# Reordering the second group of an attention-plus-MLP kernel: when a pair's mean, the weights' splits and the gates' multiplication are queued

## The chip, the cores and the metric

The kernel runs on one core of one Trainium2 chip. The metric is the device time of one execution in microseconds (us), the median of several runs. The profile is one execution of the program on the chip, taken by the hardware profiler. Its engine names are used here: PE is TensorE, DVE is VectorE, ACT is ScalarE, SP issues nearly all the transfers. Each engine works through its own instructions in the order in which the program lists them.

## The reference

```python
batch, n_heads, seq, head_dim = (8, 8, 576, 64)      # q, k, v
n_tokens, d_model, d_ff = (4608, 512, 2048)

kv  = np.einsum('bhsd,bhse->bhde', k, v)             # no softmax: 64 x 64 per head
out = np.einsum('bhsd,bhde->bhse', q, kv)
rms = np.sqrt(np.mean(out * out, axis=-1, keepdims=True) + 1e-06)
x   = out / rms * g_norm                             # then (B,H,S,D) -> (B*S, H*D)

h  = x @ w_in
sp = np.maximum(h, 0.0) + np.log1p(np.exp(-np.abs(h)))   # softplus
g  = h * erf(sp)                                     # "the gates"
y  = g @ w_out
```

Attention without a softmax gives each head a 64 x 64 matrix, an RMS norm follows, and the result is the input of a two-layer MLP. `w_in` and `w_out` arrive as 64-bit floats and are turned into 32-bit ones on the chip.

## The kernel before, in words

**Tiling.** The tokens are worked in nine groups T = 0 to 8 of 512: the first 512 tokens of each of the eight batch entries, and at last the 8 x 64 tokens left over. The hidden dimension is cut into 16 blocks (`FC`) of 128. The heads are taken as four pairs p = 0 to 3 (`NP`), a pair filling 128 partitions. While the MLP of group T runs, the attention of group T + 1 is worked in pieces between its matmuls.

**Steps.** The first two groups (`FIRST`) go through a loop of steps n = 0 to 32; T, f = divmod(n, 16). A step makes the hidden block f of its group ("the product of the step"), takes it out of PSUM, starts its softplus, and then multiplies an older block, n - 5 (`LAG`), by `w_out` into four PSUM banks ("the projection", `project`, L502). Erf runs once in four steps (f = 3, 7, 11, 15) for four blocks, since softplus and erf need different ACT tables. The later groups go through another loop, which the change does not touch.

In the second group (T = 1, n = 16 to 31) the product changes its kind from f = 2 on (`hidden`): eight matmuls of x's upper and lower parts go into a bank `n_ps`, four of a sum of both into `m_ps`. ACT copies `n_ps` with a scale to `h` (L684, "the gates' copy"), DVE adds `m_ps` to it (L427, "the add"), ACT takes the softplus (L686). `n_ps` and `m_ps` are the same two banks in every step (`turns=False`), so the next step's product can't start before the copy has read `n_ps`, nor reach its last four matmuls before the add has read `m_ps`. "The gates' multiplication" `hs[done] * ss[done]` (L644, done = n - 4) is on DVE; the projection of the next step is the first to need it.

**Weights' splits.** The second group also cuts the weights into three parts each for the later groups: `w_upper` on ACT (L411) in step f for two or three blocks (`to_cut`), `w_lower` on DVE (L414, L417) a step later, then a store to DRAM from the SP queue.

**Pieces of the attention.** For each pair, `attention` gives six pieces:

- products: kv on PE (L281), transposes of q (L303); DVE copies kv to `bd_kv` (L296), ACT copies q (L304)
- apply: q times kv on PE (L309); ACT squares it (L312)
- halve: DVE splits the squares in two (L322, L323), for group 2 and later; sq_hi and sq_lo
- mean: matmuls with a matrix of 1/64 (L330, L331; in group 1 L335); ACT loads the table of Ln and Exp (L105), Ln, Exp, Square (L342 to L344), then loads the softplus table (L108)
- norm: three DVE instructions (L350, L353, L362)
- split: x into three parts, one instruction on ACT (L387), two on DVE (L390, L393), for group 2 and later

**What sets the order.** The order is written out by hand (`manual_schedule`): an engine's queue is the order of the program. `pieces_of(T)` puts each piece in one of three places of a step: 0 is ahead of the step's product, 1 is behind softplus and the weights' cutting but ahead of the projection, 2 is behind the projection. The PSUM pool `ps_at` has two banks, which kv, the transposed q, `se_ps` and the means take in turn: the next pair's products need what the previous pair's norm has read.

In the first group the DVE also turns the 64-bit weights into 32-bit ones (`w_split` L197, L206, `w_join` L216, L220, L230).

Of the kernel before, what the change touches and what calls it, by code (L numbers as in the profile page):

```python
# [44 lines left out]
ALU = mybir.AluOpType  # L45
# [5 lines left out]
BATCH = 4  # L51
# [3 lines left out]
FIRST = 2  # L55
# [5 lines left out]
def kernel(  # L61
# [10 lines left out]
    nc = tc.nc  # L72
# [6 lines left out]
    NP = H // 2  # L79
    KC = DM // P  # L80
    FC = DF // P
# [61 lines left out]
    for i in range(2):  # L143
        nc.gpsimd.dma_start(
            out=g_col[i * D : i * D + D, :], in_=g_norm.rearrange("(d one) -> d one", one=1)
# [94 lines left out]
    def w_next(what):  # L240
        i = w_at[what]
        if i < len(w_order):
            w_at[what] = i + 1
            {"load": load_w, "split": w_split, "join": w_join}[what](*w_order[i][1:])

    def weights():

        w_next("split")
        w_next("join")
        w_next("load")  # L250
# [162 lines left out]
    def lower_w(x, high, low, both):  # L413
        nc.vector.scalar_tensor_tensor(  # L414
            out=low, in0=high.bitcast(FP32), scalar=SHIFT, in1=x, op0=ALU.mult, op1=ALU.subtract
        )
        nc.vector.tensor_tensor(  # L417
            out=both, in0=high.bitcast(FP32), in1=low.bitcast(FP32), op=ALU.subtract
        )
# [33 lines left out]
    w_kept, w_new, w_now = {}, {}, {}  # L453
# [19 lines left out]
    def w_lower(which, f):  # L473

        t, x, parts = w_new.pop((which, f))
        lower_w(x, *(parts[:, i] for i in range(3)))
        kept = w_kept[which, f] = dram.tile([P, 3, G], FP32, name=f"w_{which}{f}")
        for i in range(3):
            if t is None:
                nc.sync.dma_start(  # L480
                    out=kept[:, i].rearrange("p (c f) -> p c f", c=KC), in_=parts[:, i].bitcast(FP32)
                )
        if t is not None:
            nc.sync.dma_start(out=kept, in_=t.bitcast(FP32))
            if which == "in" and f >= WHOLE:
                w_now[which, f] = [t]
# [94 lines left out]
    def pieces_of(T):  # L581

        steps = [([], [], []) for _ in range(FC)]
        for p in range(NP):
            products, apply, halve, mean, norm, split = attention(T, p)
            short = T < FIRST or p == NP - 1
            f = (BATCH - 1) * (p + 1) if T < FIRST else BATCH * p
            steps[f][1].append(products)  # L590
            steps[f + 1][1].append(apply)
            steps[f + 2][0].append(halve)
            with_erf = short and (f + 2) % BATCH == BATCH - 1

            place = 2 if T < FIRST and p == 0 else 1 if short else 0
            steps[f + 3 - short][place].append(partial(mean, table=not with_erf))
            steps[f + 4 - short][0].append(norm)
            steps[f + 5 - 2 * short][0].append(split)
        return steps


# [11 lines left out]
    hs, ss, plain = {}, {}, {}  # L613
    whole = FIRST * FC - BATCH

    def due(k):

        i = w_at["join"] + k
        ahead = 1 if LAG - 2 <= n < LAG + BATCH else 2
        return i < len(w_order) and w_order[i][0] <= n + ahead  # L620

    for n in range(FIRST * FC + 1):
        T, f = divmod(n, FC)
        if n == FC:
            early_room.close()
            late = ctx.enter_context(tc.tile_pool(name="late", bufs=1))
            x_new = ctx.enter_context(tc.tile_pool(name="x_new", bufs=1))
            acc = ctx.enter_context(tc.tile_pool(name="acc", bufs=1))
            w_in_p = ctx.enter_context(tc.tile_pool(name="w_in_p", bufs=BATCH))
            low = low_room.enter_context(tc.tile_pool(name="low", bufs=1))  # L630
            forms = late.tile([P, 3, KC, G], FP32R, name="x_forms0")
            x_forms[FIRST] = [forms[:, i] for i in range(3)]
        if T < FIRST:
            if f == 0:
                steps = pieces_of(T + 1)
            if due(1):
                weights()
            for piece in steps[f][0]:
                piece()
        while due(0):  # L640
            weights()
        done = n - LAG + 1
        if 0 <= done < whole:
            nc.vector.tensor_tensor(out=hs[done], in0=hs[done], in1=ss[done], op=ALU.mult)  # L644
        if T == FIRST - 1:
            if f == 0:
                x_high = wide.tile([P, KC, G], FP32R, name="x_high", tag="h")
                x_low = low.tile([P, KC, G], FP32R, name="x_low")
                for i in range(0, KC, 2):
                    upper(xT[T][:, i : i + 2], x_high[:, i : i + 2])  # L650
                for i in range(0, KC, 2):
                    lower_only(xT[T][:, i : i + 2], x_high[:, i : i + 2], x_low[:, i : i + 2])
            for key in list(w_new)[:2]:
                w_lower(*key)
        if T == FIRST - 1 and f >= WHOLE:
            n_ps, m_ps = hidden(T, f, turns=False)
        elif T < FIRST:

            if n > 1:
                plain[n] = ps_h.tile([P, G], FP32, name="h_ps", tag="h")  # L660
                blocks = [(n, c) for c in range(KC)]
            elif n == 0:
                for i, (pool, tag) in enumerate(((ps_at, "at"), (ps_o, "o0"))):
                    plain[i] = pool.tile([P, G], FP32, name="h_ps", tag=tag)
                blocks = [(i, c) for c in range(KC - 1) for i in range(2)] + [(0, KC - 1)]
            else:
                blocks = [(1, KC - 1)]
            for i, c in blocks:
                nc.tensor.matmul(  # L669
                    plain[i],  # L670
                    lhsT=w_in_sb[:, c, i % FC * P : i % FC * P + P],
                    rhs=xT[T][:, c, :],
                    start=(c == 0),
                    stop=(c == KC - 1),
                )
        if T < FIRST:
            if n == whole:
                old_h = acc.tile([P, BATCH, G], FP32, name="h", tag="e")
            h = hs[n] = old_h[:, n - whole] if n >= whole else unit("h_sb")
            s = ss[n] = unit("s_sb")  # L680
            if n in plain:
                nc.scalar.copy(h, plain.pop(n))
            else:
                nc.scalar.activation(h, n_ps, AF.Copy, scale=SHIFT - 1.0)  # L684
                add(h, m_ps)
            nc.scalar.activation(s, h, AF.Softplus)  # L686
            if T == FIRST - 1:
                if f == 1:
                    x_both = wide.tile([P, KC, G], FP32R, name="x_both", tag="h")
                    for i in range(0, KC, 2):  # L690
                        both_only(x_high[:, i : i + 2], x_low[:, i : i + 2], x_both[:, i : i + 2])
                    x_forms[T] = x_high, x_low, x_both
                for key in list(w_new):
                    w_lower(*key)
                for key in to_cut[f]:
                    w_upper(*key)
            if n == 0:
                w_next("split")
            for piece in steps[f][1]:
                piece()  # L700
            if f % BATCH == BATCH - 1:
                for i in range(n - BATCH + 1, n + 1):
                    nc.scalar.activation(ss[i], ss[i], AF.Erf)
                softplus_table()
            if T == FIRST - 1:
                load_parts("in", {FC - 3: 2, FC - 2: 1, FC - 1: 1}.get(f, 0))
        if n >= LAG:
            T2, f2 = divmod(n - LAG, FC)
            last = n - LAG in (FC - 1, whole - 1)
            project(f2, hs[n - LAG], last)  # L710
            if last:
                sums(*((acc, "e") if T2 < FIRST - 1 else (wide, "h")))
                if T2 == 0:
                    for j in range(J):
                        store(T2, j, es.pop(j))
        if T < FIRST:
            for piece in steps[f][2]:
                piece()
    for n in range(whole, FIRST * FC):
        nc.vector.tensor_tensor(out=hs[n], in0=hs[n], in1=ss[n], op=ALU.mult)  # L720


    low_room.close()
# [41 lines left out]
    for m in range(first_batch, batches + 1):  # L765
        T, b = divmod(m, NB)
# [8 lines left out]
        def piece():  # L775
            if todo:
                todo.pop(0)()
# [20 lines left out]
        g, done = g_next, len(g_next)  # L798
# [25 lines left out]
        for j in range(J):  # L824
# [5 lines left out]
            for half in range(2) if j == 1 and m < batches - 1 else (j,) if j < 2 and m == batches - 1 else ():  # L830
                nc.vector.tensor_tensor(  # L831
                    out=part(h, half), in0=part(h, half), in1=part(s, half), op=ALU.mult
# [38 lines left out]
```

## Time and profile before

| | before |
|---|---|
| time, median of 3 runs | 963.03 us (961.88 to 963.95) |
| span of the profiled execution | 960.2 us |
| PE busy | 934.6 us (97%) |
| DVE busy | 740.9 us (77%) |
| ACT busy | 615.8 us (64%) |
| mean DMA rate | 271 GB/s |
| mean granted TensorE clock | 0.996 |

Share and busy time are over the whole span. The change touches the first two groups, which lie between about 28 us (the first product) and 264.5 us (the end of the last projection); the second group's steps begin at 138.7 us. Whatever moves in that stretch has to be read from that stretch: from the list of PE's waits, from the timelines of PE, DVE and ACT, and from the windows (busy time and granted clock of a stretch). In a timeline the columns are start, duration, engine, line, operation, what it writes and reads, and in square brackets the idle time ahead of it on its engine with what ended that idle time.

### The profile page before, as it was taken

How to read it: one execution, taken by the hardware profiler on the slowest of the kernel's cores; microseconds unless marked ns; L12 is line 12 of the kernel's file. 1: busy time of each engine (PE TensorE's matmuls, PEld its weight loads, DVE VectorE, ACT ScalarE, POOL GpSimd, SP SyncE). 2: the span in 40 equal slices, each digit the busy share in tenths (PEclk: the TensorE clock that was granted, in tenths of full speed). 3: DMA queues.
4: the chain of work that ended last, by engine and by line, in shares of the span. 5: the costliest groups of instructions: out<-in, count | busy, mean ns of one | idle time of the engine just before them, and what ended most of it. 6: DMA issues, size and time to landing. Idle time of an engine off the chain costs nothing.

```text
span 960.2 us, 11900 instructions
## 1 busy us (share of the span) xinstructions
PE 934.6 (97%) x4384; PEld 688.9 (72%) x4384; DVE 740.9 (77%) x1054; ACT 615.8 (64%) x825; POOL 2.4 (0%) x10
## 2 busy tenths in 40 slices
PE   6989999988999999999999999999999999999998
PEld 4444445655588787888788878888888787878886
DVE  3979957777577777888888788777777777778667
ACT  3889875577575666666666666666666666665552
POOL 0000000000000000000000000000000000000000
PEclk9999999999999999999999999999999999999999
DMA  9856506788789985998679876987697769767972
GB/s 270 266 163 215 159 1 233 269 288 309 274 318 355 367 290 190 299 379 303 250 250 376 312 272 234 352 320 288 220 371 261 263 210 367 286 264 270 368 274 65
DMA packets 110106, 259.79 MB, mean 271 GB/s; under 512 B 44256, under 2 KB 67808, under 8 KB 110048
## 3 DMA queue, kind: packets, MB, share of 16 engines
q1 hardware_dynamic: 108416, 256.73, 75.5%
q10 hardware_dynamic: 1568, 2.29, 0.8%
q8 instruction: 35, 0.57, 0.2%
q14 instruction: 23, 0.19, 0.1%
q0 software_dynamic: 64, 0.00, 0.0%
HBM read 224.40 MB, written 34.60 MB: 270 GB/s over the span
## 4 chain that ended last, share of the span: by engine, by line
PE 76%; ACT 10%; DVE 9%; DMA 2%; issue 2%; DVEq 0%; ACTq 0%
PE n_ps L444 38%; PE m_ps L444 19%; PE o_ps L502 6%; PE h_ps L669 4%; PE se_ps L309 2%; PE kv_ps L281 2%; PE qt_ps L303 1%; ACT w_new L411 1%; ACT L105 1%; DVE h L427 1%; DMA w_out_parts<-w_out 1%; ACT L108 1%; DVE e L427 1%; PE ms_ps L335 1%; DVE h L831 1%
## 5 line engine op out<-in xcount | busy, mean ns | idle before, releaser
L444 PE MATMUL n_ps<-x_forms,w_in_parts 128*128 128x512 f32 x896 | 233.9, 402 | 1.1 <-DVE x_forms L390 1.0
L444 PE MATMUL n_ps<-w_out_parts,g_forms 128*128 128x512 f32 x928 | 231.5, 391 | 0.8 <-DMA w_out_parts<-w_out 0.8
L444 PEld LDWEIGHTS n_ps<-w_out_parts,g_forms 128*128 128x128 f32 x928 | 174.1, 188 | 39.6 <-issue 1.7
L444 PEld LDWEIGHTS n_ps<-x_forms,w_in_parts 128*128 128x128 f32 x896 | 166.7, 188 | 46.0 <-issue 9.6
L815 ACT ACTIVATE s<-h 128x512 f32<-128x512 f32 x112 | 71.1, 634 | 177.2 <-DVE h L427 177.2
L427 DVE TENSOR_TENSOR h<-m_ps,h 128x512 f32<-128x512 f32 x116 | 79.8, 688 | 58.5 <-ACT h L813 42.4
L444 PE MATMUL m_ps<-w_out_parts,g_forms 128*128 128x512 f32 x464 | 124.2, 389 | 0.0
L444 PE MATMUL m_ps<-x_forms,w_in_parts 128*128 128x512 f32 x448 | 120.0, 390 | 0.0
L502 PE MATMUL o_ps<-w_out_sb,h_sb 128*128 128x512 f32 x224 | 100.5, 592 | 0.0
L444 PEld LDWEIGHTS m_ps<-w_out_parts,g_forms 128*128 128x128 f32 x464 | 87.1, 188 | 18.1
L444 PEld LDWEIGHTS m_ps<-x_forms,w_in_parts 128*128 128x128 f32 x448 | 84.1, 188 | 17.6
L427 DVE TENSOR_TENSOR e<-m_ps,e 128x512 f32<-128x512 f32 x116 | 80.2, 692 | 17.8 <-PE m_ps L444 10.9
L422 DVE SCALAR_TENSOR_TENSOR e<-n_ps,e 128x512 f32<-128x512 f32 x88 | 60.3, 685 | 41.4 <-PE n_ps L444 41.4
L502 PEld LDWEIGHTS o_ps<-w_out_sb,h_sb 128*128 128x128 f32 x224 | 42.0, 190 | 47.1 <-issue 45.4
L390 DVE TENSOR_TENSOR g_forms<-h,g_forms 128x1024 fp32r<-128x1024 f32 x58 | 70.6, 1217 | 2.9 <-ACT g_forms L387 2.6
L393 DVE SCALAR_TENSOR_TENSOR g_forms<-g_forms 128x1024 fp32r<-128x1024 f32 x58 | 71.1, 1226 | 2.0
L813 ACT ACTIVATE h<-n_ps 128x512 f32<-128x512 f32 x112 | 65.6, 585 | 8.2 <-PE se_ps L309 4.3
L387 ACT ACTIVATE g_forms<-h 128x1024 fp32r<-128x1024 f32 x58 | 58.9, 1060 | 12.5 <-PE m_ps L444 9.8
L831 DVE TENSOR_TENSOR h<-h,s 128x1024 f32<-128x1024 f32 x56 | 65.9, 1218 | 0.7 <-ACT s L819 0.7
L669 PE MATMUL h_ps<-xT,w_in_sb 128*128 128x512 f32 x144 | 64.8, 594 | 0.7 <-DVE w_in_sb L230 0.6
L108 ACT ACT_TABLE_LOAD x44 | 56.5, 1283 | 0.8
L819 ACT ACTIVATE s<-s 128x1024 f32<-128x1024 f32 x56 | 56.2, 1052 | 0.3
(98 smaller groups left out, 1028.2 us busy)
## 6 DMA issues: line engine op xcount, KB each, us to landing
w_out_parts<-w_out SPq DMA_DIRECT2D x116, 768.0 KB, 7.7
w_in_parts<-w_in SPq DMA_DIRECT2D x112, 768.0 KB, 6.5
w_in<-w_new SPq DMA_DIRECT2D x16, 768.0 KB, 3.7
k_sb<-in_k_dram SPq DMA_DIRECT2D x29, 288.0 KB, 5.8
v_sb<-in_v_dram SPq DMA_DIRECT2D x29, 288.0 KB, 5.2
q_sb<-in_q_dram SPq DMA_DIRECT2D x32, 256.0 KB, 5.5
w_raw<-in_moe_w_out_dram SPq DMA_DIRECT2D x8, 1024.0 KB, 5.4
out_dram<-e SPq DMA_DIRECT2D x32, 256.0 KB, 3.8
```

The costliest lines, as they stand in the source:

```text
L108: nc.scalar.preload_act_table_set("softplus")
L387: nc.scalar.activation(high, x, AF.Copy, scale=1.0 + 2.0**-13)
L390: nc.vector.tensor_tensor(out=low, in0=x, in1=high.bitcast(FP32), op=ALU.subtract)
L393: nc.vector.scalar_tensor_tensor(out=both, in0=low.bitcast(FP32), scalar=SHIFT, in1=high.bitcast(FP32), op0=ALU.mult, op1=ALU.add,)
L422: nc.vector.scalar_tensor_tensor(out=out_, in0=ps, scalar=scale, in1=out_, op0=ALU.mult, op1=ALU.add)
L427: nc.vector.tensor_tensor(out=out_, in0=ps, in1=out_, op=ALU.add)
L444: nc.tensor.matmul(ps, lhsT=weights(form, k), rhs=moving(form, k), start=(form == forms[0] and k == 0), stop=(form == forms[-1] and k == 3),)
L502: nc.tensor.matmul(o_ps[j], lhsT=g[:, j * P : j * P + P], rhs=w_out_sb[:, f, :], start=(f == 0), stop=last,)
L669: nc.tensor.matmul(plain[i], lhsT=w_in_sb[:, c, i % FC * P : i % FC * P + P], rhs=xT[T][:, c, :], start=(c == 0), stop=(c == KC - 1),)
L813: nc.scalar.activation(h[:, i], n_ps, AF.Copy, scale=SHIFT - 1.0)
L815: nc.scalar.activation(s[:, i], h[:, i], AF.Softplus)
L831: nc.vector.tensor_tensor(out=part(h, half), in0=part(h, half), in1=part(s, half), op=ALU.mult)
```

## The change

In `pieces_of` the pieces of a pair are placed as follows, before and after. A number is the step within the group, the second one the place in it.

| piece | second group, pairs 0 to 2 (f = 4p) before | after | pair 3 (f = 12) before | after |
|---|---|---|---|---|
| products | f, 1 | f, 2 | f, 1 | f, 2 |
| apply | f+1, 1 | f+1, 1 | f+1, 1 | f+1, 1 |
| halve | f+2, 0 | f+2, 0 | f+2, 0 | f+2, 0 |
| mean | f+3, 0 | f+2, 1 | f+2, 1 | f+2, 1 |
| norm | f+4, 0 | f+3, 0 | f+3, 0 | f+3, 0 |
| split | f+5, 0 | f+4, 0 | f+3, 0 | f+3, 0 |

So a mean comes a step sooner and behind the gates' copy of its step. In the first group (f = 3, 6, 9, 12) only the products of pair 1 move, from place 1 of step 6 to place 2; its pieces have no split.

On DVE, in the second group, the first two `w_lower` of a step go ahead of the step's place 0, and the gates' multiplication goes from ahead of the step's product to behind its add. In the first group the multiplication stays where it was. No instruction is added or taken away; the purpose is to have the instructions on which PE's next product waits come sooner in the queues of ACT and DVE.

```diff
@@ pieces_of @@
             products, apply, halve, mean, norm, split = attention(T, p)
-            short = T < FIRST or p == NP - 1
             f = (BATCH - 1) * (p + 1) if T < FIRST else BATCH * p
-            steps[f][1].append(products)
+            steps[f][2 if T == FIRST or p == 1 else 1].append(products)
             steps[f + 1][1].append(apply)
             steps[f + 2][0].append(halve)
-            with_erf = short and (f + 2) % BATCH == BATCH - 1
-            place = 2 if T < FIRST and p == 0 else 1 if short else 0
-            steps[f + 3 - short][place].append(partial(mean, table=not with_erf))
-            steps[f + 4 - short][0].append(norm)
-            steps[f + 5 - 2 * short][0].append(split)
+            with_erf = (f + 2) % BATCH == BATCH - 1
+            place = 2 if T < FIRST and p == 0 else 1
+            steps[f + 2][place].append(partial(mean, table=not with_erf))
+            steps[f + 3][0].append(norm)
+            steps[min(f + 4, FC - 1)][0].append(split)
@@ the loop of the steps @@
             if due(1):
                 weights()
+            for key in list(w_new)[:2]:
+                w_lower(*key)
             for piece in steps[f][0]:
                 piece()
@@
-        if 0 <= done < whole:
-            nc.vector.tensor_tensor(out=hs[done], in0=hs[done], in1=ss[done], op=ALU.mult)
+        if T == 0 and done >= 0:
+            gates(done)
@@
-            for key in list(w_new)[:2]:
-                w_lower(*key)
@@ behind the add and the softplus, second group only @@
+                gates(done)
                 for key in list(w_new):
                     w_lower(*key)
```

In this `pieces_of(T)` the argument is the group whose attention is worked, so T == FIRST is the attention of group 2, worked during the second group's steps.

More of the change, by code (lines that the diff above doesn't have):

```diff
@@ L620, in due, with gates @@
         return i < len(w_order) and w_order[i][0] <= n + ahead
+    def gates(n):
+        nc.vector.tensor_tensor(out=hs[n], in0=hs[n], in1=ss[n], op=ALU.mult)
     for n in range(FIRST * FC + 1):
@@ L719 @@
     for n in range(whole, FIRST * FC):
-        nc.vector.tensor_tensor(out=hs[n], in0=hs[n], in1=ss[n], op=ALU.mult)
+        gates(n)
     low_room.close()
```

## The prediction, on record before the changed kernel ran

> **What bounds the kernel now.** I read the page first: PE is busy 97% of the span, so a change can only give back PE's gaps. Then the list of PE's waits in the second group (140 to 260 us):
>
> ```profile
> PE n_ps L444 <- ACT h_sb L684: 5.5, 2, 2.8
> PE m_ps L444 <- DVE h_sb L427: 0.2, 1, 0.2
> ```
>
> Two waits make 5.5 us, each for the gates' copy on ACT. PE's timeline has them at 199.18 us (step 24) and 231.50 us (step 28). Next ACT and DVE ahead of the first:
>
> ```profile
> 186.66 0.43 DVE L322 CAST sq_hi<-qT 128x512 fp32r<-128x512 f32 x1 [2.61 <-ACT qT L312]
> 187.12 0.69 DVE L323 TENSOR_TENSOR sq_lo<-qT,sq_hi 128x512 fp32r<-128x512 f32 x1
> 187.73 0.68 DVE L644 TENSOR_TENSOR h_sb<-h_sb,s_sb 128x512 f32<-128x512 f32 x1
> ...
> 190.99 0.68 DVE L427 TENSOR_TENSOR h_sb<-m_ps,h_sb 128x512 f32<-128x512 f32 x1
> ...
> 191.71 0.63 ACT L686 ACTIVATE s_sb<-h_sb 128x512 f32<-128x512 f32 x1 [4.59 <-DVE h_sb L427]
> ...
> 193.91 1.28 ACT L105 ACT_TABLE_LOAD   x1
> ...
> 197.24 1.28 ACT L108 ACT_TABLE_LOAD   x1
> 198.53 0.60 ACT L684 ACTIVATE h_sb<-n_ps 128x512 f32<-128x512 f32 x1
> ...
> 199.18 0.79 PE L444 MATMUL n_ps<-x_high,w_new 128*128 128x512 f32 x1 [2.83 <-ACT h_sb L684]
> ```
>
> The product of step 22 is done at 185.6, but its add runs at 190.99, behind a halve that waited for ACT's Square, the gates' multiplication and two `w_lower`. Softplus, three `w_upper` and the whole mean (193.91 to 198.52) wait behind that add, and step 23's copy behind the mean. PE then has nothing.
>
> The windows (columns: PE, PEld, DVE, ACT, POOL busy, granted clock, DMA share, GB/s) show the aftermath:
>
> ```profile
> 199.00:203.00 4.00, 3.82 (x11) 3.06 (x12) 3.74 (x6) 3.21 (x6) 0.00 (x0) 0.60 1.02 365
> 231.00:236.00 5.00, 4.50 (x16) 3.16 (x18) 4.17 (x7) 4.21 (x7) 0.00 (x0) 0.69 1.01 334
> ```
>
> The granted clock is 0.60 and 0.69 after the two stalls, so they cost more than their idle time. Last, the first group, step 6:
>
> ```profile
> 62.61 0.92 PE L281 MATMUL kv_ps<-v_sb,k_sb 96*64 96x64 f32 x24 [1.88 <-DVE qT L350]
> 64.12 0.66 PE L303 MATMUL qt_ps<-ident,q_sb 128*128 128x128 f32 x4 [0.59 <-DVE xT L362]
> ```
>
> Pair 1's products wait 2.5 us for pair 0's norm, with a projection behind them that needs no norm.
>
> **What the Trainium skill says.** "TensorE: Matmul & The Clock Gate", Part 1, puts the clock at half rate after an idle window of about 3.4 us and until a busy one. The trace agrees in kind: 2.83 us idle was followed by 0.60; but the 1.88 us in step 6 was not (kv_ps took its usual 0.92). "ScalarE: Activation LUTs", What ACT_TABLE_LOAD costs, gives about 1283 ns for a load plus 1380 ns of draining; the trace shows 1.28 and the next activation 1.30 after the load's start, so no drain, and I use 1.29. "Perfetto Trace Analysis", Tensor Engine Instruction, says that ACT and DVE are strict FIFOs: one waiting instruction holds all behind it, as at 186.66.
>
> **The change part by part.** Durations are start to start from the timelines. DVE: add 0.60, gates' multiplication 0.60, `w_lower` 1.33, halve 1.07, norm 2.12, split 1.33, `bd_kv` copies 0.45. ACT: copy 0.59, softplus 0.53, `w_upper` 0.52, table 1.29, Ln to Square 2.02, four erfs 2.2, split 0.53. PE: product 2.79, projection 3.43 (so 6.22 a step), products 1.34 or 1.47, apply 1.08, mean 0.46.
>
> *What is lost before.* The last four matmuls of the product start at 156.88 in step 18 and 256.61 in step 31: 99.73 us. Work in between is 13 x 6.22 = 80.9, four means 1.8, products 4.15, applies 3.2, sum 90.1. So 9.6 us are lost; the stalls explain 5.5 + 0.2, and the rest is the slow clock.
>
> *Mean at step f+2, place 1.* On ACT this is the old position, since only the projection, which has no ACT work there, lies between. On PE the means come 3.4 us sooner; ACT's Ln had not waited for them at 195.21, so this alone gives about 0.1 us. They now need the halve by the product's end.
>
> *`w_lower` first, gates last on DVE.* This is what moves the add. In step 22 two `w_lower` (2.7) fill what was idle ahead of the halve and the multiplication (0.6) goes behind: add at about 188.2 instead of 190.99. On the clock of before, for steps 22 to 24: add 188.2, softplus to 189.4, three `w_upper` to 190.9, mean to 195.5, copy of step 23 done at 196.1. PE: product 22 ends 187.3, mean, projection, product 23 from 191.95, projection, product 24 wants to start at 198.2. Slack 2 us: the stall goes, and the slow clock with it. The pattern of step 26 to 28 gives 224.2 against 226.3: slack again 2 us. The multiplication is needed only by the next step's projection, over 2 us later: free.
>
> *Split at f+4.* Free on PE for pair 3, but for pairs 0 and 1 the split's ACT part now comes behind four erfs and a table load, and DVE's part waits in front of the add. In step 20 ACT's table ends at 173.7, split 174.3; DVE has been idle since 170.5 and then does split to 175.7, add 176.3, multiplication 176.9, third `w_lower` 178.2, two copies of the sums (L529, now ahead) 179.4, `bd_kv` 179.9. Before, `bd_kv` was copied at 176.17, ahead of the sums.
>
> *Products at place 2.* They are 3.4 us later, and apply follows right behind the next product. PE ends product 21 at 178.3 and apply waits for `bd_kv` until 180.0: a new stall of 1.7 us, with the projection behind it. By step 6 above I take no slow clock from it; if there is one, it is some 1.5 us. In step 22 the mean waits for the halve until 188.3 instead of 187.5 (0.8). In steps 25 and 26 `bd_kv` and the halve are 0.1 and 0.2 late; step 24 has no sums on DVE. New stalls: 1.7 + 0.8 + 0.3 = 2.8 us.
>
> *Second group:* 9.6 - 2.8 = 6.8 us.
>
> *First group, pair 1 behind the projection.* That fills the 2.5 us. But DVE is busy without a gap from 61.87 to over 110 us, and PE runs into it: `bd_kv` only at 69.8 (1.7 left), the weights of step 8 only at 74.6 (h wanted at 76.0: 1.4 left), and pair 2's transposes need the norm that ends at 87.86. PE had them at 88.27:
>
> ```profile
> 87.11 0.75 DVE L362 SCALAR_TENSOR_TENSOR xT<-se_ps,gm_col,qT 128x512 f32<-128x512 f32 x1
> ...
> 88.27 0.60 PE L303 MATMUL qt_ps<-ident,q_sb 128*128 128x128 f32 x4
> ```
>
> So 0.4 us remain. Sum: 6.8 + 0.4 = 7.2 us.
>
> *Behind the group* nothing is owed: the last `w_in` parts and x's split stand to the last projection as before (DVE's last multiplications begin 0.15 us before its end both ways), and between 260 and 800 us PE's waits are 0.7 us. A transfer rate up by 6% where the DMA share is 0.83 to 0.94 might cost a little; I take none, one us at most.
>
> **The rivals.**
> A. As worked out: 963.0 - 7.2 = 955.8 us.
> B. VectorE keeps up better than I queue it (no stall at step 21, mean not waiting), and the first group keeps 0.4 to 1: 9.6 + 0.4 = 10 us, 953 us. For it: my largest new stall rests on one queue position, the sums. Against: that position is plain in the order of the program.
> C. ACT stays the bound: it carries both a mean (4.6) and an erf block (4.8) within two steps of 6.2 us, so one of the two stalls comes back with its slow clock (4.5): 963.0 - 2.7 = 960.3 us. For it: at step 20 the copy has only 0.8 us of slack. Against: 2 us of slack where the stalls were.
> D. Slower: the new queue behind the erfs stalls PE over the clock's window at steps 21 and 25, and both old stalls stay: 2.8 on top, 965.8 us. Against: step 25 has no sums ahead of `bd_kv`.
>
> **How the numbers follow.** A 0.62, B 0.13, C 0.16, D 0.09. Predicted is A. The range holds A with both bounds (1.5 for a slow clock, 1 for transfers, 2.8 if no new stall comes), most of B and about half of C: 952.3 to 960.0. Faster by over 0.2% (below 961.1) is A, B and most of C: 0.85; within 0.2% 0.07; slower 0.08.
>
> **What would show it.** PE's waits on L684 in the second group gone, granted clock near 1.0 from 190 to 240 us; the add of step 22 within a microsecond of the halve; a new wait of some 1.7 us at L308 for `bd_kv` in step 21 and 0.8 at L330/L331 in step 22; in the first group no wait at step 6, small ones at steps 7, 8 and 9. Wrong would be a wait on L684 that is still there, a slow clock behind the step-21 stall, or a gain in the second group that the later groups give back.

## The result and the profile after

The changed kernel takes 957.27 us (957.07 to 957.74) where the kernel before takes 963.35 us (961.88 to 963.95) in the same session: ratio 0.994, 95% interval 0.9923 to 0.9957. The forecast was 955.8 us, 7.2 us less; it is 6.1 us less. So direction and range hold and the gain is somewhat smaller. The reasons turned out to be only partly the right ones.

The list of PE's waits in the first group (40 to 139 us), then in the second (140 to 262 us), of the kernel after:

```profile
PE kv_ps L308 <- DVE bd_kv L296: 0.8, 1, 0.8
PE qt_ps L303 <- DVE xT L362: 0.3, 1, 0.3
PE kv_ps L281 <- DVE qT L350: 0.3, 1, 0.3
...
PE kv_ps L308 <- DVE bd_kv L296: 1.4, 1, 1.4
PE se_ps L309 <- ACT qT L304: 0.7, 1, 0.7
PE o_ps L502 <- DVE h_sb L622: 0.3, 1, 0.3
PE ms_ps L330 <- DVE sq_hi L322: 0.3, 1, 0.3
PE ms_ps L331 <- DVE sq_lo L323: 0.2, 1, 0.2
```

The two waits of 2.8 us for the gates' copy are gone. The waits that the forecast put in their place are there: step 21's apply for `bd_kv` (1.4 us, forecast 1.7) and step 22's mean for the halve (0.3 and 0.2). Two it did not have are there as well: 0.7 us for q's copy in step 25 and 0.3 us for the gates' multiplication. The windows of the kernel after (columns as before: five engines' busy time, then the granted clock):

```profile
176.00:190.00 14.00, 12.09 (x41) 7.15 (x41) 13.23 (x25) 7.59 (x15) 0.00 (x0) 1.00 0.84 282
192.00:215.00 23.00, 22.29 (x97) 13.70 (x96) 18.35 (x32) 18.63 (x29) 0.00 (x0) 1.00 0.95 341
220.00:236.00 16.00, 16.00 (x76) 9.76 (x75) 12.13 (x20) 13.33 (x19) 0.00 (x0) 1.00 0.93 338
```

The clock stays at 1.00, after the new wait of step 21 too. The timeline of DVE shows why the copy is no longer late (step 22: halve, add, multiplication) and where the new wait comes from (step 20: split behind 3.73 us of idling, and `bd_kv` behind all the rest):

```profile
174.63 0.69 DVE L390 TENSOR_TENSOR x_forms<-x,x_forms 128x512 fp32r<-128x512 f32 x1 [3.73 <-ACT x_forms L387]
...
178.49 1.28 DVE L529 COPY e<-o_ps 128x512 f32<-128x512 f32 x2
179.69 0.45 DVE L296 COPY bd_kv<-kv_ps 64x64 f32<-64x64 f32 x2
...
187.97 0.69 DVE L323 TENSOR_TENSOR sq_lo<-qT,sq_hi 128x512 fp32r<-128x512 f32 x1
188.58 0.68 DVE L427 TENSOR_TENSOR h_sb<-m_ps,h_sb 128x512 f32<-128x512 f32 x1
189.18 0.68 DVE L622 TENSOR_TENSOR h_sb<-h_sb,s_sb 128x512 f32<-128x512 f32 x1
```

**Where the time went, step by step.** The start of the last four matmuls of a product (`m_ps`, L444) marks each step. The table gives the distance from the mark of one step to that of the next in us, in the profiles of this study. The shortest distances seen sum to 90.1 us, the same as the forecast's sum of work.

| steps | before | after | DVE order only | DVE order, products late | front |
|---|---|---|---|---|---|
| 18 to 20 | 12.88 | 12.85 | 12.87 | 12.87 | 12.86 |
| 20 to 21 | 7.65 | 7.64 | 8.73 | 7.63 | 7.65 |
| 21 to 22 | 7.28 | 8.97 | 7.28 | 7.58 | 7.44 |
| 22 to 23 | 7.04 | 7.68 | 6.67 | 6.69 | 7.15 |
| 23 to 24 | 10.78 | 6.21 | 6.20 | 6.72 | 6.19 |
| 24 to 25 | 7.77 | 7.75 | 11.88 | 7.85 | 7.75 |
| 25 to 26 | 7.29 | 8.21 | 7.30 | 7.73 | 7.57 |
| 26 to 27 | 6.70 | 7.01 | 6.67 | 6.67 | 6.99 |
| 27 to 28 | 9.64 | 6.21 | 6.21 | 6.20 | 6.21 |
| 28 to 29 | 8.72 | 7.63 | 9.72 | 7.73 | 7.65 |
| 29 to 31 | 13.98 | 13.95 | 13.98 | 13.97 | 13.97 |
| 18 to 31 | 99.73 | 94.11 | 97.51 | 91.64 | 91.43 |

The second group loses 9.6 us before and 4.0 us after: 5.6 us won, against 6.8 forecast. The two profiles differ by 4.3 us (960.2 and 955.9): 5.6 won in these steps, 0.3 lost ahead of them (the first k and v arrived 0.6 us later in this execution, 0.3 of it won back in the first group), 1.0 lost behind them, of which 0.6 lie in step 32. From profile to profile the stretch behind step 31 varies by 1.4 us, so the rest of it is not put down to the change. The medians differ by 6.1 us: the profiled execution of the kernel before (962.1 us) was faster than its median, that of the changed kernel (957.7 us) slower.

### The profile page after: what moved, and what is told of

Same layout as the page of the kernel before. It is cut to its first block, busy times and chain, and to the rows that moved or that the text cites. A ratio compares the mean times of both kernels' runs of the same rounds, so it can differ in the third digit from the quotient of the medians.

```text
span 955.9 us, 11913 instructions
## 1 busy us (share of the span) xinstructions
PE 932.4 (98%) x4384; PEld 685.9 (72%) x4384; DVE 740.4 (77%) x1054; ACT 616.3 (64%) x825; POOL 2.4 (0%) x10
## 4 chain that ended last, share of the span: by engine, by line
PE 76%; ACT 10%; DVE 9%; DMA 3%; issue 2%; SPq 0%; DVEq 0%
PE n_ps L444 40%; PE m_ps L444 20%; PE o_ps L502 5%; PE h_ps L671 3%; PE se_ps L309 2%; PE kv_ps L281 2%; PE qt_ps L303 1%; ACT L105 1%; DMA w_raw<-in_moe_w_in_dram 1%; ACT s_sb L706 1%; DMA w_out_parts<-w_out 1%; DMA w_out<-w_new 1%; DVE h L427 1%; DMA v_sb<-in_v_dram 1%; ACT w_e L205 1%
## 5 line engine op out<-in xcount | busy, mean ns | idle before, releaser
L444 PE MATMUL n_ps<-x_forms,w_in_parts 128*128 128x512 f32 x896 | 233.9, 402 | 1.1 <-DVE x_forms L390 1.0
L444 PE MATMUL n_ps<-w_out_parts,g_forms 128*128 128x512 f32 x928 | 231.6, 391 | 1.0 <-DMA w_out_parts<-w_out 1.0
L444 PEld LDWEIGHTS n_ps<-w_out_parts,g_forms 128*128 128x128 f32 x928 | 174.1, 188 | 39.7 <-issue 1.7
L444 PEld LDWEIGHTS n_ps<-x_forms,w_in_parts 128*128 128x128 f32 x896 | 166.7, 188 | 46.2 <-issue 9.6
L444 PE MATMUL m_ps<-w_out_parts,g_forms 128*128 128x512 f32 x464 | 124.2, 389 | 0.0
L444 PE MATMUL m_ps<-x_forms,w_in_parts 128*128 128x512 f32 x448 | 120.1, 390 | 0.0
L444 PEld LDWEIGHTS m_ps<-w_out_parts,g_forms 128*128 128x128 f32 x464 | 87.1, 188 | 18.1
L444 PEld LDWEIGHTS m_ps<-x_forms,w_in_parts 128*128 128x128 f32 x448 | 84.1, 188 | 17.6
```

Of the source, the lines that this page charges most:

```text
L444: nc.tensor.matmul(ps, lhsT=weights(form, k), rhs=moving(form, k), start=(form == forms[0] and k == 0), stop=(form == forms[-1] and k == 3),)
```

## The experiments

Each edit is given against the kernel named. Times are medians in us; the ratio is to the kernel before on the same chip in the same session.

### The two halves of the change, each alone

Pieces alone: the new `pieces_of`, DVE's order as before.

```diff
# against the changed kernel
-            for key in list(w_new)[:2]:     # ahead of place 0
-                w_lower(*key)
-        if T == 0 and done >= 0:
+        if 0 <= done < whole:
             gates(done)
+            for key in list(w_new)[:2]:     # behind the multiplication
+                w_lower(*key)
-                gates(done)                 # behind the add
```

> The new places of the pieces alone (products, mean, norm, split, first group too), with VectorE's order as before (halve, gates' multiplication, two w_lower, then the add). Theory: what cost the time was the add's place in VectorE's queue, and moving the pieces alone puts even more in front of it in step 20 (split behind the erfs, then multiplication and two w_lower). So no gain, rather slower than before: 964 to 968 us, a wait of 2 us or more at or ahead of step 21's apply, and waits for the gates' copy or the add still there in steps 23 to 28. Rival: the mean a step sooner is the gain, then about 957 us, no wait for the gates' copy.

Measured: 978.9 us, ratio 1.0166 (1.0153 to 1.0179). The first lines of the list of PE's waits in the second group:

```profile
PE n_ps L444 <- DVE w_new L414: 6.7, 5, 1.7
PE n_ps L444 <- ACT h_sb L686: 4.7, 3, 2.1
...
```

Slower, as expected, but by 15 us and not by some 3. What was missing in the expectation is the first line: `w_lower` of a step makes the parts that the next step's product reads. Behind the split, which waits behind the erfs, they come so late that PE waits for them too. The pieces' new places without `w_lower` first are much worse than no change at all.

DVE's order alone: the old `pieces_of`, first group as before.

```diff
# against the kernel before
+            for key in list(w_new)[:2]:     # ahead of place 0
+                w_lower(*key)
-        if 0 <= done < whole:
+        if T == 0 and done >= 0:
             gates(done)
-            for key in list(w_new)[:2]:
-                w_lower(*key)
+                gates(done)                 # behind the add
```

> VectorE's order alone (two w_lower first, multiplication behind the add), pieces where they were before, first group as before. Theory: the whole gain of the second group or a little more, 955.5 to 957.5 us; both stalls of 2.8 us at steps 24 and 28 under 1 us, no stretch at a clock of 0.6, no wait of 1.4 us for bd_kv in step 21. Rival (the mean's place matters): at least one stall of over 2 us stays, 959.5 to 962 us.

Measured: 961.7 us, ratio 0.9981 (0.9973 to 0.9989): 1.8 us less. That is not what the theory said; it is in the rival's range, but not for the rival's reason. From the list of PE's waits in the second group, and the windows around step 24:

```profile
PE kv_ps L281 <- DVE u L350: 4.1, 3, 2.5
PE qt_ps L303 <- DVE x L362: 1.2, 2, 0.6
...
196.00:203.00 7.00, 4.54 (x20) 2.78 (x20) 5.94 (x10) 6.18 (x11) 0.00 (x0) 1.00 0.98 356
203.00:207.00 4.00, 4.00 (x32) 3.06 (x31) 3.48 (x8) 3.23 (x5) 0.00 (x0) 0.57 0.78 288
```

The stalls at the gates' copy are all gone, so DVE's order does what it was expected to do. But in steps 20, 24 and 28 the next pair's products now wait for the previous pair's norm, which is queued on DVE in the same step, and behind the longest of these waits (2.46 us, step 24) the slow clock follows again (0.57). The stall changed its place: 23 to 24 fell from 10.78 to 6.20 us, 24 to 25 rose from 7.77 to 11.88.

The new order itself puts the norm back: the multiplication and two `w_lower` now stand between the add of step 19 and the norm of step 20. DVE's timeline has this add and this norm, first in the kernel before, then in this one:

```profile
165.87 0.69 DVE L427 TENSOR_TENSOR h_sb<-m_ps,h_sb 128x512 f32<-128x512 f32 x1 [3.14 <-ACT h_sb L684]
166.47 0.68 DVE L350 SCALAR_TENSOR_TENSOR u<-ms_ps,u 128x512 f32<-128x512 f32 x1
...
166.54 0.69 DVE L427 TENSOR_TENSOR h_sb<-m_ps,h_sb 128x512 f32<-128x512 f32 x1 [3.14 <-ACT h_sb L687]
...
171.11 0.68 DVE L350 SCALAR_TENSOR_TENSOR u<-ms_ps,u 128x512 f32<-128x512 f32 x1
```

The norm starts 0.60 us behind the add before and 4.57 us here; in steps 24 and 28 it is 1.93 us before and 5.20 us here. In those two steps PE was also late before: it came to the products at 203.54 and 235.75 us, just behind norms that ended at 203.29 and 235.61. How much of the new waits there belongs to which is not shown by a run; in step 20 PE had no stall before, so there it is the order alone. My theory fell here: the add's place is necessary, and not enough.

### What the pieces are needed for

DVE's order alone, and in addition only the products behind the projection. Mean, norm and split stay where they were, the first group too.

```diff
# against the kernel with DVE's order alone
-            steps[f][1].append(products)
+            steps[f][2 if T == FIRST else 1].append(products)
```

> VectorE's order alone (as in the run that had only that), and in addition the second group's products behind the projection; mean, norm and split stay where they were before, first group as before. Theory: with VectorE's order alone PE lost its time in steps 20, 24 and 28, where the products waited 0.9, 2.5 and 1.9 us for the norm queued in the same step (and a slow clock behind 2.5 us); the projection of 3.4 us fills these waits, so the time is that of the changed kernel, 956.5 to 958.5 us, with no wait for L350 or L362 in the second group. Rival: the norm is late whatever PE does meanwhile, and the waits move to apply (bd_kv, q's copy) a step later, 960 us or more.

Measured: 955.5 us, ratio 0.9911 (0.9896 to 0.9926). PE's waits in the second group:

```profile
PE o_ps L502 <- DVE h_sb L623: 0.3, 1, 0.3
PE n_ps L444 <- ACT h_sb L687: 0.2, 1, 0.2
PE se_ps L309 <- ACT qT L304: 0.2, 1, 0.2
```

The projection fills the wait for the norm. This kernel is at least as fast as the full change, although it leaves the mean, norm and split in their places and leaves out the first group's part. In the table it loses 1.5 us over the second group, the changed kernel 4.0. This order together with the first group's part was not run.

The mean a step sooner, undone in the changed kernel; the norm stays where the change put it.

```diff
# against the changed kernel
-            steps[f + 2][place].append(partial(mean, table=not with_erf))
+            if T == FIRST and p < NP - 1:
+                steps[f + 3][0].append(partial(mean, table=not with_erf))
+            else:
+                steps[f + 2][place].append(partial(mean, table=not with_erf))
```

> The changed kernel with the means of pairs 0 to 2 back in place 0 of step f+3, ahead of the norm, which stays where the change put it. Theory: ACT's queue is the same in both, since nothing of ACT lies between the two places, so the norm is not later; PE's waits for the halve in step 22 (0.26 and 0.22 us) go and others grow by as much or less: 956.5 to 957.5 us. Rival: the mean a step sooner is what brings the norm in time, then waits of PE for the norm or the copy come back, 959 us or more.

Measured: 956.9 us, ratio 0.9938 (0.9926 to 0.9951), the same as with the change. Steps 22 to 23 take 6.69 us and no longer 7.68, and other waits grew instead. The mean's own place gains nothing.

The products back ahead of the projection, in the changed kernel.

```diff
# against the changed kernel
-            steps[f][2 if T == FIRST or p == 1 else 1].append(products)
+            steps[f][2 if T < FIRST and p == 1 else 1].append(products)
```

> The changed kernel with the second group's products back in place 1 (ahead of projection and sums). The apply of step 21 no longer waits for bd_kv behind the sums' copies: its wait of 1.43 us falls to about 0.4. Theory: VectorE is what bounds steps 20 to 22, so step 22's mean, which waits for the halve, waits the more (0.5 to about 1.5 us) and the time stays within 0.6 us of the changed kernel's 957.3. Rival: the queue position was all, the time falls by 1 us or more, and the mean's wait stays 0.5.

Measured: 956.7 us, ratio 0.9936 (0.9923 to 0.9948). From the list of PE's waits in the second group:

```profile
PE ms_ps L330 <- DVE sq_hi L322: 1.3, 1, 1.3
...
PE kv_ps L308 <- DVE bd_kv L296: 0.2, 1, 0.2
```

The wait for `bd_kv` fell from 1.4 to 0.2 us and the mean's wait rose from 0.3 to 1.3: what step 21 gains, step 22 loses. I read this as DVE bounding the stretch, so that PE's order only chooses the step in which PE pays. With the norm a step sooner, the products' place does not matter; with the norm where it was, it is worth 6 us. The norm sooner and the products later are two cures of one thing. (The split moved together with the norm in all these runs; the two were not tried apart.)

### The two parts of DVE's order

The multiplication back ahead of the product, in the changed kernel.

```diff
# against the changed kernel
-        if T == 0 and done >= 0:
+        if 0 <= done < whole:
             gates(done)
-                gates(done)                 # behind the add
```

> The changed kernel with the gates' multiplication back ahead of the product (w_lower still first). Theory: the add comes 0.6 us later in each step, and ACT's copies behind it had about 2 us of slack in steps 23 and 27, about 1 us in steps 20 and 24, so within 0.8 us of the changed kernel: 957 to 958 us, no stall over 1 us for the gates' copy. Rival (the multiplication's place is what frees the add): the stalls at the copy come back, 960 us or more.

Measured: 960.0 us, ratio 0.997 (0.9959 to 0.9981): 2.7 us slower than the change, where 0.8 had been the most expected. No stall at the gates' copy came back, so the rival is out as well. From PE's timeline of step 21, the window behind it, and the list of PE's waits in the second group:

```profile
179.88 0.43 PE L308 MATMUL kv_ps<-qT_last,bd_kv 128*128 128x64 f32 x2 [1.69 <-DVE bd_kv L296]
180.15 1.79 PE L309 MATMUL se_ps<-qT,bd_kv 128*128 128x512 f32 x2
181.74 4.66 PE L502 MATMUL o_ps<-w_out_sb,h_sb 128*128 128x512 f32 x8
...
180.00:185.00 5.00, 5.00 (x10) 2.22 (x11) 3.96 (x7) 1.63 (x4) 0.00 (x0) 0.66 1.07 331
...
PE se_ps L309 <- ACT qT L304: 2.2, 2, 1.3
```

The wait for `bd_kv` grew only from 1.43 to 1.69 us, but in this profile the granted clock fell to 0.66 behind it: the apply takes 1.79 us for 1.08, the projection 4.66 for 3.60, together 1.8 us more. That is not what makes the kernel slower, though. Two of its seven executions have a mean granted clock of 1.000, which leaves no room for such a stretch (5 us at 0.66 lower the mean by 0.002), and they take 959.4 and 960.0 us like the others. The rest of the profile shows a likelier cause: PE now waits for q's copy 1.34 us in step 25 (0.71 in the changed kernel) and 0.81 us in step 29 (none). On ACT this copy stands behind the softplus, and the softplus waits for the add, which the multiplication now precedes: in steps 23 and 24 the softplus begins 2.16 and 2.78 us behind the start of the gates' copy, in the changed kernel 1.56 and 2.18.

The two `w_lower` back behind the pieces, in the changed kernel.

```diff
# against the changed kernel
-            for key in list(w_new)[:2]:     # ahead of place 0
-                w_lower(*key)
+            for key in list(w_new)[:2]:     # behind place 0, ahead of the product
+                w_lower(*key)
```

> The changed kernel with the two w_lower back behind the pieces of place 0 (multiplication still last). Theory: this is the part that the new places of the pieces need: in step 20 w_lower waits behind the split, which waits behind the erfs, so the parts of the weights that step 21's product reads come some 2 us late, and the add is 2.7 us later in steps 20, 22, 24; waits of PE for w_lower (L414) in steps 21, 25 and 29 with slow clock behind them, 965 to 974 us. Rival: it is the multiplication's place that counts, 957 to 959 us.

Measured: 975.5 us, ratio 1.0131 (1.0117 to 1.0145). PE waits 3.3 us in four places for `w_new` (L414) and 5.9 us in four for the gates' copy, with a slow clock behind them; steps 20 to 21 take 12.45 us. So `w_lower` first is the part without which the pieces' new places bring a loss.

### The first group's part

```diff
# against the kernel before
-            steps[f][1].append(products)
+            steps[f][2 if T < FIRST and p == 1 else 1].append(products)
```

> Only the first group's pair 1 products behind the projection of step 6. Theory: VectorE bounds steps 6 to 9, so the stretch from step 6's product (57.14 us before) to step 16's product (138.66 us before, 81.52 us) gets 0.3 to 0.4 us shorter, with waits at steps 7, 8 and 9 in place of the 2.5 us at step 6; the second group's two stalls as before. Rival: the 2.5 us are kept, a stretch of about 79 us.

One execution, 962.9 us. PE's waits in the first group are those of the changed kernel (0.8, 0.3 and 0.3 us), not the 2.5 us of step 6. From step 6's product (57.27) to step 16's (138.50) it is 81.23 us against 81.52: 0.29 us won, as forecast from DVE's queue. The profile before has no slow clock behind step 6; where there is one, the wait costs more (last section).

### Using DVE's idle time behind the erfs

In step 20 of the changed kernel DVE idles for 3.73 us and is then late for two steps. Here `w_lower` (the third too) and the multiplication go ahead of the pieces in steps 20, 24 and 28, and the products are back in place 1.

```diff
# against the changed kernel with the products in place 1
-            for key in list(w_new)[:2]:
+            early_gates = T == FIRST - 1 and f > 0 and f % BATCH == 0
+            for key in list(w_new)[: None if early_gates else 2]:
                 w_lower(*key)
+            if early_gates:
+                gates(n - LAG + 1)
...
-                gates(done)
+                if not early_gates:
+                    gates(done)
```

> Products of the second group in place 1 as before, and in steps 20, 24 and 28, where VectorE idles behind the erfs, all w_lower and the gates' multiplication ahead of the pieces. Theory: VectorE's 3.7 us of idle time in step 20 takes 1.9 us of its work, bd_kv and the halve come 1.9 us sooner, and PE's waits in steps 21 and 22 (1.9 us in the changed kernel) fall to about 0.6 in sum: 955.3 to 956.3 us. Rival: ACT, not VectorE, sets steps 21 and 22 (copy of q behind the sums, Square), waits as before, 957 us.

Measured: 953.6 us (953.39 to 954.82), ratio 0.991 (0.9894 to 0.9925), the shortest time of this study and faster than both kernels; it gained more than expected. PE's waits in the second group:

```profile
PE o_ps L502 <- DVE h_sb L622: 0.3, 1, 0.3
PE ms_ps L331 <- DVE sq_lo L323: 0.2, 1, 0.2
```

The waits of steps 21 and 25 are gone, and DVE's idle time in step 20 fell from 3.73 to 1.80 us. The second group is down to 91.43 us, 1.3 above the sum of its work.

The same with the means back in step f+3 (edit as above):

> The kernel with w_lower and multiplication in front in steps 20, 24 and 28 and the products in place 1, and in addition the means of pairs 0 to 2 in place 0 of step f+3. Theory: only the wait of 0.2 us for the halve is left to take, the same time within 0.5 us: 953.1 to 954.1 us. Rival (the mean's place matters once the other waits are gone): 955 us or more.

Measured: 954.1 us, ratio 0.9894 (0.9877 to 0.991): the intervals overlap, so again the mean's place makes no difference.

## Why the prediction was right, and where it was wrong

**What bounds the kernel.** Right, and shown by the runs. The gates' copy was late because the add stood behind the halve, the multiplication and two `w_lower`. Changing that order alone removes both stalls with nothing else moved. Of its two parts, `w_lower` first is the one that counts for the copy: in the changed kernel no stall there came back with the multiplication ahead of the add, and 5.9 us of them did with `w_lower` behind the pieces. The loss of 9.6 us before is confirmed by the steps of all profiles: the shortest distances sum to the 90.1 us of the forecast.

**"This is what moves the add": right, but not what the gain is made of.** I put the whole 9.6 us down to it. Alone it gives 1.8 us of time, since the products then wait for the norm. The forecast walked the queue for the add and left out the norm of the second group: that `w_lower` first and the multiplication last put a norm in the same step 3 to 4 us further behind the add. The full change is spared this because its norm comes a step sooner, for which the forecast gave no value; that part of the forecast came out by luck.

**"Products at place 2 … a new stall": the stall was right, its price was not.** The stall was there (1.43 us for 1.7), and I counted the move as a cost of that size. In the changed kernel, where the norm also comes sooner, undoing it only moves the wait to the next step and leaves the time as it is. With DVE's order alone it is a gain: it turns 961.7 into 955.5 us.

**"Mean at step f+2 … about 0.1 us": right.** Undoing it leaves the time the same, twice. What is left of the pieces' move is the norm a step sooner (with the split), and the products' move alone does as much.

**Split at f+4.** Its mechanism was right: the split waits behind the erfs (3.73 us of idle DVE in step 20) and everything behind it is late in steps 20 to 22. The forecast named pairs 0 and 1; it is so for pair 2 in step 28 too. Filling that idle time removed the waits. With `w_lower` behind the pieces, the split among them, the time is 975.5 us.

**New waits mis-sized: 2.8 forecast, 4.0 measured.** In us: steps 21 to 22 1.7 (forecast 1.7), 22 to 23 1.0 (0.8), 25 to 26 0.9 (0.1), 26 to 27 0.3 (0.2). The term that is off is step 25. In step 22 ACT's second `w_upper` waited 0.54 us for a `w_new` buffer whose store was still under way; ACT's timeline of the changed kernel:

```profile
190.99 0.63 ACT L411 ACTIVATE w_new<-w_out_sb 128x512 fp32r<-128x512 f32 x1 [0.54 <-DMA w_out<-w_new]
```

That store was issued at 183.96 us, in SP's queue behind the stores of the sums and the loads of the next pair, and the DMA share from 180 to 190 us is 1.03 to 1.07. The kernel before had no such wait, and I had taken none; q's copy in step 25 came as much later. That the 0.54 us make up most of the 0.71 us is read from the order on ACT, not shown by a run of its own. The run with DVE's idle time used and the means back speaks against it as the whole cause: there PE waits 0.56 us for the same copy, and ACT waits for no store. Why step 25 was put too low stays open in part.

**The multiplication "needed only by the next step's projection, over 2 us later: free": wrong in step 32.** There the projection follows with no product between, and waits for it; 7.53 us for the last two projections against 6.95 before, 0.6 us lost. In the other direction its place mattered more than the 0.8 us that I expected before that run: moving it back costs 2.7 us, by its profile mostly through the softplus behind the add.

**Slow clock: right, but not for the reason given.** I took none behind the new stall, and there was none (the mean clock is 0.999 or 1.000 in all four executions). My reason was that the 1.88 us of step 6 had brought none. The same wait brought one in two other profiles (last section), so this was in part luck.

**First group.** Forecast 0.4 us, measured 0.3; the waits came at steps 7 and 9 as worked out, and none at step 8.

## What to carry to other kernels

When an instruction goes ahead in a queue, everything that it passes comes later: here two `w_lower` and the multiplication freed the add and put back the norm. Redo the whole queue for each instruction that another engine waits for, and redo it with the old stall gone, since with PE 3 us late other inputs look in time. Where an engine must idle behind a long neighbour (here DVE behind four erfs and a table load), put work that is already due ahead of the waiting instruction; in the changed kernel that was worth about 3 us, where moving the products or the mean was worth nothing. Parts of a reordering can be harmful alone and good together, so test them singly before keeping all: here the mean's move carried nothing.

## What the runs showed of the hardware

The length of a wait alone does not decide whether the clock falls behind it. Idle waits of PE of 2.83 and 2.46 us were followed by a granted clock of 0.60 and 0.57, and one of 1.69 us by 0.66 over the next 5 us; 1.43 us at the same place in the changed kernel was not, nor 1.52 us there with the mean back in step f+3. Step 6 of the first group shows it most plainly. The same products wait there for the same norm in the kernel before (1.88 us), in the one with DVE's order alone (1.87 us) and in the one with the products late too (1.90 us). The windows behind that wait, in this order:

```profile
64.00:68.00 4.00, 3.88 (x12) 2.02 (x13) 3.97 (x6) 3.26 (x5) 0.00 (x0) 1.00 0.00 0
64.00:68.00 4.00, 4.00 (x9) 1.77 (x8) 3.97 (x5) 3.40 (x5) 0.00 (x0) 0.68 0.21 15
64.00:68.00 4.00, 4.00 (x11) 2.10 (x10) 3.97 (x5) 3.67 (x5) 0.00 (x0) 0.73 0.00 0
```

The projection behind it takes 3.60, 4.83 and 4.36 us, and from step 6's product to step 16's it is 81.52, 83.16 and 82.71 us. So in an execution where the clock falls there, this wait costs 1.2 to 1.6 us more, and taking it away, as the change does, is worth more than the 0.3 us seen against the profile before. How often that happens in the kernel before is not on record.

The Trainium skill, "TensorE: Matmul & The Clock Gate", Part 1, speaks of an idle window of about 3.4 us; the run with 1.69 us is half of that, and the measurement decides. What else decides, the neighbouring gaps or where the window happens to lie, was not tried.
